# Nineteen small extra loads at the start of a one-core decode kernel that streams a key and value cache

## The chip, the cores and the metric

The kernel runs on one core of a Trainium2 chip. The metric is the time of one execution in microseconds (us), the median of repeated runs. A core has a matrix engine (TensorE, "PE" in the profile), a vector engine (VectorE, "DVE"), a scalar engine (ScalarE, "ACT"), GpSimd ("POOL") and SyncE ("SP"), which here only issues transfers. Sixteen DMA engines move data between the large memory (HBM) and the on-chip buffer (SBUF). An engine issues a transfer with one instruction; the instruction goes on a queue, and the DMA engines work through the queue's pieces ("packets"). In the profile, "SPq" is SyncE's stream of such instructions.

## What is computed

One token goes through two branches, whose results are mixed with a scalar gate. The reference, cut to what matters:

```python
g = sigmoid((x * gate_w).sum(-1))                      # x: 1 x 1 x 448
q = (x @ wq).reshape(16 heads, 256)                    # wq: 448 x 4096
scores = q . k_cache * 256 ** -0.5                     # k_cache: 8 heads x 65536 x 256, bf16
a = (softmax(scores) . v_cache).reshape(4096) @ wo     # two query heads share one key/value head
b = (relu(x @ W_gate) * (x @ W_up)) @ W_down           # 448 -> 1792 -> 448
out = g * a + (1 - g) * b
```

The two caches have 268 MB each. Everything else together is about 12 MB.

## The kernel before

**Tiles.** Each of the 8 key/value heads is cut into 4 tiles of the key cache and 4 of the value cache. A tile is 128 partitions x 32768 bf16 elements, 64 KB in each partition and 8.39 MB in all. There are 64 tiles. Three SBUF buffers, `ring[0]` to `ring[2]`, take the tiles in turn; a tile's load is issued when the buffer's last user is done with it. For a key tile, VectorE transposes blocks in place (line 352, eight pieces), TensorE multiplies with the query (line 364), VectorE takes the maximum (line 501) and ScalarE the exponential (line 503). For a value tile TensorE multiplies with the transposed probabilities (line 395). The last value tile comes in four pieces, and the output weights `wo` are spread over the end (line 579).

**The order of the work.** Each operation is noted with an engine, a due time and its dependencies (`op` and `dma`). At the end each engine's operations are sorted by due time and written out in that order, with waits on counters (semaphores) ahead of an operation that needs another engine's or a transfer's result. So the due time fixes the place in an engine's program, and nothing else. An engine that waits holds up all that comes after it in its own program.

**The start, in SyncE's order.** The order of issue is: `wq` (384 of the 448 rows of the query weights, into `ring[2]`, line 434), the gate and up weights (384 rows each, line 449), `wqh` (the other 64 rows of the query weights, into `ring[1]`, line 435), the first key tile into `ring[0]` (line 495), then the last 64 rows of gate and up as 32 transfers of 4 rows each (`rows64`, line 375), the down weights (`wd`, line 482), and the key tiles 1 and 2. `rows64` waits for `z_f`, a GpSimd memset of the padding (line 243), the first operation in GpSimd's program. `wd` waits for the query product `q` (line 324), because it overwrites the query weights in `ring[2]`. Key tile 1 goes into `ring[1]` and waits for `q` as well, since `wqh` lies there; key tile 2 goes into `ring[2]` and waits for the gated branch (`gu`, `dn`).

**GpSimd at the start.** After `z_f` it makes index and selection tables (lines 260 to 275). The last of them, `selc`, is read by a transpose on TensorE (line 443) right after `q`.

The dictionary `held` lists, for each ring buffer, what must be done before its first tile is loaded.

Of the kernel before, what the change touches and what calls it, by code (L numbers as in the profile page):

```python
# [24 lines left out]
class _Plan:  # L25
# [8 lines left out]
    def op(self, eng, key, fn, deps=()):  # L34
        o = _Op(eng, key, fn, deps)
        self.ops.append(o)
        return o

    def dma(self, eng, key, sem, fn, deps=()):
        if sem not in self.dsem:  # L40
            self.dsem[sem] = self.es.enter_context(self.nc.semaphore("d_" + sem))
        o = _Op(eng, key, fn, deps, dma=sem)
        self.ops.append(o)
        return o
# [46 lines left out]
def bass_gated_mix__gqa_block_cached__glu_gated_reglu__decode_kernel(  # L91
# [38 lines left out]
    with es:  # L130
# [3 lines left out]
        ring = [sb("ring%d" % i, [128, U * DH], BF) for i in range(NRING)]  # L134
# [61 lines left out]
        op, dma = pl.op, pl.dma  # L196
        touch_m = []

        def mop(*a, **k):
            o = op(*a, **k)  # L200
            touch_m.append(o)
            return o
# [18 lines left out]
        t = 3.0  # L221
# [5 lines left out]
        T_END = t + 20.0  # L227


        slot, held, freed = {}, {1: ["q"], 2: ["gu", "dn"]}, {}  # L230
        r = 0
        for kind, i, _ in order:
            if kind in ("k", "v") or (kind, i) in (("wo", 0), ("vp", 0)):
# [145 lines left out]
        l_, qk, smax, aexp, pv, last = {}, {}, {}, {}, {}, {}  # L379
# [52 lines left out]
        for kind, i, t in issue:  # L432
            if kind == "wq":
                l_["wq"] = dma("sp", t, "wq", lambda e: e.dma_start(wq3, A_wq[0:NR3, :].rearrange("(p k) n -> p (k n)", k=R3)))
                l_["wqh"] = dma("sp", t + 0.01, "wqh", lambda e: e.dma_start(
                    wqa, A_wq[NR3:D, :].rearrange("r (c n) -> (r c) n", c=2)))
                tq = tL["wq", 0]
                l_["qm"] = mop("pe", tq, f_q, [l_["wq"], q0])
                l_["q"] = mop("pe", tq + 8, f_q2, [l_["qm"], l_["wqh"]])
# [5 lines left out]
            elif kind == "gu":  # L445
                a1, a2 = [], []
                t = tL["gu", 0]
# [43 lines left out]
            elif kind == "k":  # L491
# [14 lines left out]
                if t_ == NTH - 1:  # L506
# [13 lines left out]
                    for rd in range(2):  # L520
# [18 lines left out]
                        q = op("ac", tt + 1, f_ev, [p, pv.get((h - 1) * NTH - 1)])  # L539
# [103 lines left out]
```

## Time and profile before

| | |
|---|---|
| time, median of 2 runs | 1281.05 us (1280.99 to 1281.1) |
| the profiled execution's own time | 1281.17 us |
| its span, first to last instruction | 1279.9 us |
| read from HBM | 549.03 MB, 429 GB/s over the span |
| PE, DVE, ACT, POOL busy | 33%, 50%, 5%, 1% of the span |

The span is what the profiler saw of the program; 1.27 us of that execution's time lie outside it. The share of a DMA queue is the time that its packets took, as a share of sixteen engines' span. The windows of the profile count a packet in the window in which it starts, so that in a short window the share can be over 1. A transfer's landing is counted from its issue to the last rise of its semaphore.

### The profile page before, as it was taken

To read this page: it belongs to the slowest core of one execution; us is meant where nothing else is said; L and a number is where in the kernel's file an instruction comes from. 1 tells how busy PE (TensorE), PEld (TensorE's weight loads), DVE (VectorE), ACT (ScalarE), POOL (GpSimd) and SP (SyncE) were. 2 spreads that over 40 slices of the span, in tenths; PEclk is the share of its full clock that TensorE was granted. 3 is DMA by queue.
4 is the path that set the end of the run, shared out by engine and by line. 5 is a ranking of instruction groups with operands and counts; after the bars stand their busy time and mean duration, and the time that the engine had idled before them with its cause. 6 is when DMAs were issued, how large, how long until landed. Compare 5 with 4: busy or idle time off the path is not lost.

```text
span 1279.9 us, 10025 instructions
## 1 busy us (share of the span) xinstructions
PE 426.5 (33%) x4634; PEld 159.5 (12%) x4634; DVE 639.1 (50%) x438; ACT 61.5 (5%) x116; POOL 10.5 (1%) x22
## 2 busy tenths in 40 slices
PE   5324323334223431325331343322433314233244
PEld 4201101111001110002110111100111101011021
DVE  2588633565434655345555444555435555336600
ACT  0000000000000000000000000000000000000000
POOL 3000000000000000000000000000000000000000
PEclk8655666656666666666656666656566666666576
DMA  9999999999999999999999999999999999999997
GB/s 410 428 427 447 429 428 433 437 433 429 439 431 431 435 435 426 433 445 427 427 433 440 435 425 431 437 439 427 427 435 441 428 431 435 435 431 437 430 426 334
DMA packets 11936, 549.68 MB, mean 429 GB/s; under 512 B 1395, under 2 KB 1654, under 8 KB 2806
## 3 DMA queue, kind: packets, MB, share of 16 engines
q1 hardware_dynamic: 11890, 549.03, 99.4%
q8 instruction: 36, 0.59, 0.2%
q14 instruction: 6, 0.05, 0.0%
q10 hardware_dynamic: 4, 0.00, 0.0%
HBM read 549.03 MB, written 0.00 MB: 429 GB/s over the span
## 4 chain that ended last, share of the span: by engine, by line
DVE 34%; DMA 31%; another core or an unknown queue 16%; PE 14%; SPq 2%; issue 1%; ACT 1%; POOL 0%; POOLq 0%
DVE ring L352 31%; DMA ring<-in_A_k_cache_dram 27%; PE ST L364 6%; PE O L395 6%; DMA ring<-in_A_wo_dram 3%; DVE P_sb L523 1%; SPq L375 1%; DMA ring<-in_B_W_up_dram 1%; DVE nmb L501 1%; PE PT L528 1%; POOL ring L243 0%; ACT ptp L537 0%; PE M_ps L515 0%; DVE attnT L425 0%
## 5 line engine op out<-in xcount | busy, mean ns | idle before, releaser
L352 DVE STREAM_TRANSPOSE ring<-ring 128x2048 uint32<-128x2048 uint32 x256 | 565.5, 2275 | 408.9 <-DMA ring<-in_A_k_cache_dram 408.9
L364 PE MATMUL ST<-ring,xm 128*16 128x512 bf16 x2048 | 225.5, 614 | 754.0 <-DVE ring L352 754.0
L364 PEld LDWEIGHTS ST<-ring,xm 128*16 128x16 bf16 x2048 | 61.6, 120 | 903.6 <-DVE ring L352 794.6
L395 PE MATMUL O<-ring,ptp 128*4 128x512 bf16 x2048 | 149.2, 455 | 34.6 <-DMA ring<-in_A_v_cache_dram 30.6
L503 ACT ACTIVATE P_sb<-ST,nmb 128x512 bf16<-128x512 f32 x32 | 45.2, 1414 | 1112.0 <-DVE nmb L501 1112.0
L501 DVE TENSOR_REDUCE nmb<-ST 128x1 f32<-128x512 f32 x32 | 22.0, 689 | 109.6 <-PE ST L364 109.6
L395 PEld LDWEIGHTS O<-ring,ptp 128*4 128x4 bf16 x2048 | 54.2, 99 | 129.3 <-issue 60.3
L409 DVE CAST o_sb<-O 128x512 bf16<-128x512 f32 x8 | 5.5, 692 | 78.2 <-PE O L395 78.2
L523 DVE TENSOR_TENSOR P_sb<-P_sb,hs 128x1024 bf16<-128x1024 bf16 x16 | 18.9, 1222 | 8.9 <-ACT hs L517 8.9
L528 PE MATMUL PT<-identb,P_sb 128*128 128x128 bf16 x128 | 16.5, 310 | 15.5 <-DVE P_sb L523 14.7
L528 PEld LDWEIGHTS PT<-identb,P_sb 128*128 128x128 bf16 x128 | 12.3, 140 | 18.3 <-DVE P_sb L523 18.3
L537 ACT COPY ptp<-PT 128x256 bf16<-128x256 bf16 x32 | 10.3, 375 | 23.0 <-PE PT L528 23.0
L317 PE MATMUL M_ps<-ring,P_sb 128*128 128x256 bf16 x48 | 8.3, 357 | 0.7 <-DMA ring<-in_A_wq_dram 0.7
L503 ACT ACTIVATION_READ_ACCUMULATOR P_sb<-ST,nmb 128x1 f32 x32 | 8.5, 267 | 0.0
L467 PE MATMUL M_ps<-xT,ring 48*128 48x1 bf16 x28 | 1.8, 195 | 14.5 <-DMA ring<-in_B_W_up_dram 14.5
L317 PEld LDWEIGHTS M_ps<-ring,P_sb 128*128 128x128 bf16 x48 | 6.0, 127 | 2.8 <-DMA ring<-in_A_wq_dram 0.7
L243 POOL MEMSET ring<- 32x7168 bf16 x1 | 6.1, 6061 | 0.3 <-POOLq L628 0.3
L513 PE MATMUL M_ps<-identf,hs 128*2 128x128 f32 x8 | 2.7, 335 | 10.0 <-DVE hs L511 10.0
L441 DVE STREAM_TRANSPOSE ptp<-P_sb 128x128 uint32<-128x128 uint32 x1 | 0.3, 311 | 11.2 <-ACT P_sb L440 11.2
L459 PE MATMUL M_ps<-xT,ring 128*128 128x1 bf16 x84 | 5.2, 198 | 1.7 <-DVE nselT L444 1.7
L425 DVE TENSOR_SCALAR attnT<-M_ps,hs 64x4 bf16<-64x4 f32 x16 | 3.5, 221 | 3.7 <-PE M_ps L418 3.6
L597 PE MATMUL A_ps<-ring,attnT 128*1 128x224 bf16 x64 | 5.3, 321 | 0.1
(78 smaller groups left out, 82.8 us busy)
## 6 DMA issues: line engine op xcount, KB each, us to landing
ring<-in_A_v_cache_dram SPq DMA_DIRECT2D x1, 4096.0 KB, 27.0
ring<-in_A_wq_dram SPq DMA_DIRECT2D x1, 3072.0 KB, 10.2
ring<-in_A_v_cache_dram SPq DMA_DIRECT2D x1, 2048.0 KB, 31.6
ring<-in_A_v_cache_dram SPq DMA_DIRECT2D x2, 1024.0 KB, 34.6
ring<-in_A_wo_dram SPq DMA_DIRECT2D x4, 448.0 KB, 36.4
ring<-in_B_W_down_dram SPq DMA_DIRECT2D x1, 1568.0 KB, 19.6
ring<-in_B_W_gate_dram SPq DMA_DIRECT2D x1, 1344.0 KB, 13.0
ring<-in_B_W_up_dram SPq DMA_DIRECT2D x1, 1344.0 KB, 15.8
```

Source lines behind the costliest of these rows:

```text
L243: z_f = op("gp", -0.5, lambda e: e.memset(ring[2][0:32, WB - 2 * F:WB + 2 * F], 0.0))
L317: ins = e.matmul(QN_ps, xw3[:, kt, 31 - j:159 - j], wq3[:, kt * NQ + j * 256:kt * NQ + (j + 1) * 256], start=(j == 0 and kt == 0), stop=Fa ...
L352: return lambda e: e.transpose(v, v)
L364: ins = e.matmul(bank[32 * w:32 * w + 16, :], xm[:, x0:x0 + 16], ktv[sl][:, u0:u0 + 16, c, :, r_], start=(b == 0 and c == 0 and r_ == 0), ...
L375: d_ = dma("sp", t + 0.0001 * i, sem, lambda e, i=i, b0=b0, r0=r0: e.dma_start(dsts[i // 8][b0:b0 + 13:4, :], W[r0:r0 + 13:4, :]), deps)
L395: ins = e.matmul(OP[h % 2][32 * g:32 * g + 4, :], ptp[h % 2][:, col:col + 13:4], ring[sl][:, k * 512:(k + 1) * 512], start=(a == 0 and k < ...
L409: e.tensor_copy(dst[:, :, 0:4, :], src)
L501: smax[n] = op("dv", tk + 22, lambda e, n=n, NM=NM, t_=t_: e.tensor_reduce(NM[:, t_:t_ + 1], ST[n % 2][:], AX.X, ALU.max, negate=True), [q ...
L503: aexp[n] = op("ac", tk + 23, lambda e, n=n, t_=t_, NM=NM, RS=RS: e.activation(P_sb[:, t_:2048:4], ST[n % 2][:], ACTF.Exp, bias=NM[:, t_:t ...
L523: rsc = op("dv", tt, lambda e, X=X, pb=pb: e.tensor_tensor(pb, pb, X[:, 12:16].unsqueeze(1).to_broadcast([128, 256, 4]), ALU.mult), [h7, a ...
L528: ins = e.transpose(PT[rd][:, s * 128:(s + 1) * 128], P_sb[:, (rd * 8 + s) * 128:(rd * 8 + s + 1) * 128], identb[:, :])
L537: ins = e.copy(dst, src)
```

## The change

Two groups of loads are added, and nothing reads what they bring.

- `pk`: 15 loads on SyncE's queue. The i-th takes i rows of `wq`, 1024 elements (2 KB) of each, into i partitions of `ring[1]`, beyond the part that `wqh` uses. Their due times lie between 3.0051 and 3.0065; `wq` has 3.0, gate and up have 3.001 and 3.002, `wqh` has 3.01. So in SyncE's program they stand behind the gate and up weights and ahead of `wqh`.
- `pg`: 4 loads on GpSimd's queue, each of 4 rows of `wq` into partitions 64 to 67 of `ring[1]`, with 8, 7, 6 and 5 KB per row. Their due times, -0.9 to -0.87, put them ahead of `z_f` (-0.5), the first operation of GpSimd's program.
- Key tile 1, the first tile in `ring[1]`, additionally waits until both groups have landed.

```diff
-        slot, held, freed = {}, {1: ["q"], 2: ["gu", "dn"]}, {}
+        slot, held, freed = {}, {1: ["q", "pk", "pg"], 2: ["gu", "dn"]}, {}
...
                 l_["wqh"] = dma("sp", t + 0.01, "wqh", lambda e: e.dma_start(
                     wqa, A_wq[NR3:D, :].rearrange("r (c n) -> (r c) n", c=2)))
+                for i in range(1, 16):
+                    l_["pk"] = dma("sp", t + 0.005 + 0.0001 * i, "pk", lambda e, i=i: e.dma_start(
+                        ring[1][0:i, 4096 + i * 1024:4096 + (i + 1) * 1024], A_wq[0:i, 0:1024]))
+                for i in range(4):
+                    l_["pg"] = dma("gp", -0.9 + 0.01 * i, "pg", lambda e, i=i: e.dma_start(
+                        ring[1][64:68, 4096 + i * 4096:8192 + i * 4096 - 512 * i], A_wq[4 * i:4 * i + 4, 0:4096 - 512 * i]))
```

## The prediction

> **What bounds the kernel now.** I read the page's queue part first, then a table of the span by stretches, then SyncE's own waits.
>
> ```profile
> q1 hardware_dynamic: 11890, 549.03, 99.4%
> HBM read 549.03 MB, written 0.00 MB: 429 GB/s over the span
> ```
>
> ```profile
> 2.00:1278.00 1276.00, 426.23 (x4634) 159.50 (x4634) 637.62 (x432) 60.65 (x115) 9.04 (x18) 0.62 1.00 431
> 1270.00:1274.00 4.00, 1.73 (x16) 0.21 (x16) 0.00 (x0) 0.00 (x0) 0.00 (x0) 0.50 0.79 318
> 1274.00:1276.00 2.00, 1.91 (x26) 0.90 (x24) 1.14 (x4) 0.00 (x0) 0.00 (x0) 0.50 0.44 174
> 1276.00:1278.00 2.00, 1.94 (x22) 0.83 (x18) 0.19 (x1) 0.00 (x0) 0.00 (x0) 0.50 0.14 53
> ```
>
> ```profile
> SPq L560 <- PE ST L364: 912.2, 29, 35.0
> ```
>
> SyncE's queue keeps the sixteen DMA engines busy for 99.4% of the span. In the stretches (the last two columns are the DMA share and GB/s) the share is 1.00 from 2 us to 1278 us; the hardware has no idle time to lose except in the last 8 us, where the share falls to 0.79, 0.44 and 0.14: some DMA engines run out of work earlier than others. SyncE itself waits 912.2 us for ring buffers to come free, which looks like the bound and isn't, as the landings show:
>
> ```profile
> ring<-in_A_v_cache_dram SPq DMA_DIRECT2D x31, 36.7
> ```
>
> A tile has 8.39 MB, which takes 8.39 / 0.429 = 19.6 us. A value tile lands 36.7 us after its issue, so it finds some 17 us of other work ahead of it in the queue. While SyncE waits, the DMA engines have work. The time is therefore set by the bytes that the DMA engines must move, plus the start and the end, and the engine with most to do ends last. A delay of an issue costs time only where it is longer than the queue that lies ahead of it.
>
> **The change, part by part.** Nothing is removed. Four things are added or moved.
>
> *1. Work for the DMA engines.* The fifteen `pk` loads have 1 + 2 + ... + 15 = 120 rows of 2048 B, 245,760 B. The four `pg` loads have 4 x (8192 + 7168 + 6144 + 5120) = 106,496 B. Together 0.352 MB, at 429 GB/s 0.82 us if all sixteen engines share it. How unevenly small loads fall is shown by the loads of 4 rows that are there already:
>
> ```profile
> 26.16 17.25 DMA ring<-in_B_W_up_dram
> ```
>
> ```profile
> 6.80 10.04 SPq L375 DMA_DIRECT2D ring<-in_B_W_gate_dram  x16
> 16.88 9.86 SPq L375 DMA_DIRECT2D ring<-in_B_W_up_dram  x16
> 38.79 6.70 DVE L352 STREAM_TRANSPOSE ring<-ring 128x2048 uint32<-128x2048 uint32 x3 [15.10 <-DMA ring<-in_A_k_cache_dram]
> 43.51 1.81 PE L467 MATMUL M_ps<-xT,ring 48*128 48x1 bf16 x28 [14.50 <-DMA ring<-in_B_W_up_dram]
> ```
>
> The first fence is from the chain that ended last, cut to the start; the second is the timeline. The 32 loads of 4 rows are queued behind key tile 0. Vector work on that tile starts at 38.79, so it had landed by then. The small loads have landed at 26.16 + 17.25 = 43.41, 4.62 us later. They hold 32 x 4 x 3584 B = 0.459 MB, which sixteen engines would move in 1.07 us and four engines in 4.28 us. So a load of 4 rows runs on four engines. The rest, 4.62 - 4.28 = 0.34 us over 32 packets on an engine, is 0.011 us of overhead per packet.
>
> If a load of i rows likewise gives one row to each of i engines, always starting from the same one, the first engine gets 15 packets of 2048 B. At 429 / 16 = 26.8 GB/s per engine each takes 0.076 + 0.011 = 0.087 us, in all 1.3 us; the fifteenth engine gets 0.09 us. For `pg` each engine gets at most one 8 KB row if the four loads go to different engines, 0.31 + 0.01 = 0.3 us, and 26,624 B, 1.0 us, if all four go to the same. The existing small loads leave four engines 4.6 us behind, and the falling shares in the last 8 us are what such a lag looks like when it is never made up: with 17 us queued, the other twelve never wait for the slow four, and the end does. If the first engine of `pk` is one of these four, the end moves by **1.3 + 0.3 = 1.6 us**. The ends of this term are 0.8 us (evenly spread) and 1.3 + 1.0 = 2.3 us. I take 1.6, nearest to what the 4-row loads show.
>
> [...] The 4.62 us agree with four engines; which four, no row here shows.
>
> *2. SyncE's issue time.* The nearest rows of issues:
>
> ```profile
> 0.72 0.40 SPq L434 DMA_DIRECT2D ring<-in_A_wq_dram  x1
> 1.63 0.43 SPq L449 DMA_DIRECT2D ring<-in_B_W_up_dram  x1
> 2.11 0.75 SPq L435 DMA_DIRECT2D ring<-in_A_wq_dram  x1
> 2.90 0.44 SPq L495 DMA_DIRECT2D ring<-in_A_k_cache_dram  x1
> 26.79 3.03 SPq L482 DMA_DIRECT2D ring<-in_B_W_down_dram  x1
> 29.86 32.37 SPq L495 DMA_DIRECT2D ring<-in_A_k_cache_dram  x3
> ```
>
> The 32 small issues went from 6.80 to 26.74, 0.62 us each. The 128-partition issues take 0.45 us with the step to the next, `wqh` 0.79. So fifteen `pk` cost between 6.8 and 11.9 us; I take the 4-row rate, 15 x 0.62 = **9.3 us**. `wqh` is then issued at 2.11 + 9.3 = 11.4 (at worst 14.0), key tile 0 at 12.2 (14.8), the small loads from 12.6 (15.2). Is there work in the queue until then?
>
> ```profile
> ring<-in_B_W_up_dram SPq DMA_DIRECT2D x1, 1344.0 KB, 15.8
> ring<-in_A_wq_dram SPq DMA_DIRECT2D x1, 512.0 KB, 16.6
> ```
>
> The up weights land at 1.63 + 15.8 = 17.4 and `wqh` at 2.11 + 16.6 = 18.7. These engines are thus occupied up to about 17 us without either, and key tile 0 is needed some 1.2 us after that. Issues at 11.4 and 12.2 are ahead by 5 us, the worst ones by 3. The query product isn't hurt: its first part runs on TensorE until 19.34, and `wqh` lands at most 1.6 us later than 18.7, with `wd` as its nearest customer more than 10 us away. Cost: nothing, covered by `wq`, gate and up.
>
> The small loads then end at 12.6 + 19.9 = 32.5, `wd` (3.03 us, a long issue that I leave as it is) at 35.6, and key tile 1 is issued at about 35.7 instead of 29.86. Key tile 0 keeps every engine busy until about 38.8 + 0.8, and `wd`'s 1.6 MB for 3.7 us more. Cost: nothing; what is left of the cover is about 4 us on twelve engines, and 4.6 us more on the four that have the small loads.
>
> *3. GpSimd.* No row shows a load issued by GpSimd. The rows around it:
>
> ```profile
> 0.72 6.06 POOL L243 MEMSET ring<- 32x7168 bf16 x1 [0.29 <-POOLq L628]
> 12.16 0.19 POOL L275 TENSOR_SCALAR selc<-selc 128x2 f32<-128x2 f32 x1
> 21.88 0.27 PE L443 MATMUL M_ps<-identf,selc 128*2 128x128 f32 x1 [0.55 <-ACT P_sb L440]
> ```
>
> The memset `z_f` ends at 6.78 now. Behind four issues of X us it ends at 6.78 + 4X. Nearest rows are SyncE's issues: 0.4 to 3.03 us. I take 1 us: `z_f` ends at 10.8, before SyncE gets to the small loads (12.6), so it is hidden behind part 2. At the upper end, X = 3.03, it ends at 18.9 and the small loads end at 38.8. Twelve engines would run dry for about 1 us before `wd`; they are the ones with 4.6 us to spare at the end. So both ends cost nothing. The tables end at 12.35 now and at 16.4 with X = 1; TensorE reads them at 21.88, and at the upper end (24.5) the gate product waits 2.6 us, with its second half waiting for data until 43.51 anyway. Through this I see no cost.
>
> [...]
>
> *4. The added wait.* Key tile 1 waits for `pk` and `pg` too. Behind it on SyncE stand all later tiles. Both groups are issued by 11.4 us and lie ahead of key tile 0 in the queue, so they have landed long before 35.7. Cost: nothing.
>
> **The sum.** 0 + 1.6 + 0 + 0 = +1.6 us on a profiled execution of 1281.17 us (span 1279.9 and 1.27 outside), so 1282.8; the median of the runs shown is 0.12 lower, which gives **1282.6 us**, 0.12% slower. A measurement of this kernel can tell about 2% from no change, so this is no change.
>
> **The rivals.**
>
> *Evenly spread.* If the small loads fall on engines that aren't the last at the end, or rotate, the added bytes alone count: 0.8 us, 1281.9. For it: the order in which engines end isn't in any row. Against it: 4-row loads go to four engines.
>
> *GpSimd is the bound of the start (slower).* Point of decision: the four late engines have work until 43.41 + 1.6 = 45.0. The small loads and then `wd` with its 3.03 us must have been issued by then, which takes 19.9 + 3.03 = 22.9 us, so `z_f` must end by 45.0 - 22.9 = 22, which is X = 3.8 us. From there each us of X costs 4 us: at X = 6 (z_f at 30.8) the loss is 8.8 us, 1291; at X = 10.4 it is 26 us, 1308, over 2%. For it: GpSimd's issue is unseen here and its memset of 32 partitions takes 6.06 us, so GpSimd is slow. Against it: no issue row is above 3.03 us.
>
> *The lag changes the rate (faster).* The `pk` loads set the engines apart in steps of 0.09 us. If engines that read less in step moved more, say 433 instead of 431 GB/s over the whole stream, 549.03 MB would take 1268 instead of 1274 us, and the time would be 1277. The best neighbouring stretches read 433 and 436:
>
> ```profile
> 142.00:182.00 40.00, 11.69 (x128) 3.75 (x128) 18.36 (x9) 1.40 (x2) 0.00 (x0) 0.64 1.00 433
> 182.00:222.00 40.00, 10.88 (x128) 3.47 (x128) 19.03 (x10) 1.42 (x2) 0.00 (x0) 0.63 1.01 436
> 222.00:262.00 40.00, 10.90 (x136) 3.79 (x136) 20.98 (x14) 1.42 (x2) 0.00 (x0) 0.59 0.99 428
> ```
>
> Against it: the 436 is paid back by 428 in the next stretch, with share 1.01 and 0.99, so this is counting at the edges and not a better rate. The engines are also out of step already, by the 4.6 us of the small loads. The same mechanism could cost as much, 1289.
>
> *The loads are dropped or merged*: 1281.05. Each has its own semaphore and key tile 1 waits for it, so I give this next to nothing.
>
> **How the numbers follow.** Forecast (skewed, hidden issues, 1281.8 to 1283.5) 0.55; evenly spread (1281.0 to 1281.8) 0.2; GpSimd as the bound 0.12, of which 0.03 over 2%; changed rate 0.12, split 0.07 faster and 0.05 slower, with 0.01 of each over 2%; dropped 0.01. The range takes in the first two, half of the faster cases and the slower ones up to X = 5.5: 1279.5 to 1289. Faster by over 2%: 0.01; within 2%: 0.95; slower by over 2%: 0.04.
>
> **What would show it.** Right: fifteen new issues on SyncE of about 0.62 us between the up weights and `wqh`, key tile 0 issued near 12 us, key tile 1 near 36 us; the DMA share of the stretches up to 60 us no lower than now; about 0.35 MB more read; the last wait for `wo` some 1.6 us later. Wrong: GpSimd issues over 3.8 us each, with VectorE waiting for key tile 1 much longer than now; a gap in the DMA share near 40 us; or a rate over the whole stream other than 431 GB/s, which no step here would explain.

## The result, and the profile after

The changed kernel took 1289.56 us (1288.52 and 1290.6), the kernel before 1281.05 us (1280.99 and 1281.1). The ratio is 1.0067, with a 95% interval of 1.005 to 1.0083: within the 2% that the prediction took as its bound, but clear of no change. Forecast was +1.6 us, measured +8.5 us, and the upper end of the range, 1289, was passed by half a microsecond. The profiled execution took 1288.52 us with a span of 1287.2 us, 7.35 us more than the one of before.

First the page of the changed kernel.

```profile
q1 hardware_dynamic: 12130, 549.28, 99.4%
q0 software_dynamic: 128, 0.11, 0.0%
HBM read 549.38 MB, written 0.00 MB: 427 GB/s over the span
```

The added 0.35 MB are there (549.38 against 549.03), and the queue's share is the same 99.4%. So the DMA engines aren't idler. Where is the time? The table by stretches tells (columns: from and to, length, busy time and count of PE, PEld, DVE, ACT and POOL, granted clock, DMA share, GB/s). Before:

```profile
2.00:14.00 12.00, 3.91 (x24) 2.85 (x25) 6.52 (x20) 0.99 (x2) 9.04 (x18) 1.00 0.91 385
14.00:28.00 14.00, 11.70 (x122) 9.69 (x121) 1.89 (x10) 0.37 (x1) 0.00 (x0) 0.85 1.11 479
2.00:82.00 80.00, 31.93 (x338) 21.57 (x338) 42.69 (x49) 2.75 (x5) 9.04 (x18) 0.72 1.01 432
82.00:1200.00 1118.00, 356.29 (x3887) 123.75 (x3891) 580.63 (x366) 54.75 (x102) 0.00 (x0) 0.61 1.00 433
```

The same stretches after:

```profile
2.00:14.00 12.00, 0.91 (x9) 0.77 (x9) 9.36 (x20) 1.00 (x2) 11.03 (x17) 1.00 0.91 327
14.00:28.00 14.00, 7.12 (x48) 5.42 (x48) 0.00 (x0) 0.00 (x0) 0.87 (x5) 0.89 1.11 335
2.00:82.00 80.00, 29.91 (x306) 21.07 (x306) 36.59 (x44) 2.77 (x5) 11.90 (x21) 0.69 1.01 395
82.00:1200.00 1118.00, 361.18 (x3915) 124.87 (x3915) 581.81 (x367) 54.62 (x102) 0.00 (x0) 0.62 1.00 433
```

From 82 us to 1200 us both kernels run at 433 GB/s. All of the loss lies before. There the *share* is the same (0.91 and 1.11 in both), and the *rate* is not: 327 instead of 385 GB/s from 2 to 14 us, 335 instead of 479 from 14 to 28 us. The engines are busy with packets that take longer: by the packet records the 256 packets of 10,752 B of the gate and up weights took 404 ns each before and 500 ns on average after, the 128 packets of 4096 B of `wqh` 159 and 377 ns. A busy share can't show this; the column beside it does. Over the first 82 us the shortfall is (432 - 395) GB/s x 80 us = 2.96 MB, at 433 GB/s 6.8 us, and with the 0.8 us for the added bytes it accounts for the 7.35 us. Packets count where they start, so this measure, used for all runs below, is uncertain by about 1 us.

The timeline of the changed kernel shows who was where:

```profile
1.25 2.29 POOL L441 DMA_DIRECT2D ring<-in_A_wq_dram  x4 [0.81 <-POOLq L634]
2.11 5.67 SPq L438 DMA_DIRECT2D ring<-in_A_wq_dram  x15
3.53 6.09 POOL L243 MEMSET ring<- 32x7168 bf16 x1
7.82 0.39 SPq L435 DMA_DIRECT2D ring<-in_A_wq_dram  x1
8.25 0.43 SPq L501 DMA_DIRECT2D ring<-in_A_k_cache_dram  x1
9.64 10.26 SPq L375 DMA_DIRECT2D ring<-in_B_W_gate_dram  x16
19.94 16.62 SPq L375 DMA_DIRECT2D ring<-in_B_W_up_dram  x16
28.05 3.57 PE L324 MATMUL M_ps<-ring,P_sb 128*128 128x256 bf16 x16 [6.45 <-DMA ring<-in_A_wq_dram]
36.61 5.25 SPq L488 DMA_DIRECT2D ring<-in_B_W_down_dram  x1
41.97 30.20 SPq L501 DMA_DIRECT2D ring<-in_A_k_cache_dram  x3
47.34 6.70 DVE L352 STREAM_TRANSPOSE ring<-ring 128x2048 uint32<-128x2048 uint32 x3 [13.35 <-DMA ring<-in_A_k_cache_dram]
```

GpSimd's four issues take 2.29 us in all and SyncE's fifteen 5.67 us, both less than assumed. Key tile 0 is issued at 8.25, far ahead of need. And yet the second part of the query product, which needs `wqh`, starts at 28.05 instead of 19.40, and the work on key tile 0 at 47.34 instead of 38.79. Issuing is early, moving is late. The line before of the second part, to compare:

```profile
19.40 1.92 PE L324 MATMUL M_ps<-ring,P_sb 128*128 128x256 bf16 x16
```

### The profile page after: what moved, and what is told of

It is laid out like the page before. It is cut to its first block, busy times and chain, and to the rows that moved or that the text cites. A ratio compares the mean times of both kernels' runs of the same rounds, so it can differ in the third digit from the quotient of the medians.

```text
span 1287.2 us, 10045 instructions
## 1 busy us (share of the span) xinstructions
PE 428.4 (33%) x4634; PEld 159.8 (12%) x4634; DVE 641.9 (50%) x438; ACT 61.4 (5%) x116; POOL 12.8 (1%) x26
## 3 DMA queue, kind: packets, MB, share of 16 engines
q1 hardware_dynamic: 12130, 549.28, 99.4%
HBM read 549.38 MB, written 0.00 MB: 427 GB/s over the span
## 4 chain that ended last, share of the span: by engine, by line
DVE 34%; DMA 31%; another core or an unknown queue 16%; PE 14%; SPq 3%; issue 1%; ACT 1%; POOL 1%; POOLq 0%
DVE ring L352 31%; DMA ring<-in_A_k_cache_dram 27%; PE ST L364 6%; PE O L395 6%; DMA ring<-in_A_wo_dram 2%; DMA ring<-in_B_W_up_dram 2%; DVE P_sb L529 1%; SPq L375 1%; SPq L585 1%; DVE nmb L507 1%; PE PT L534 1%; POOL ring L243 0%; ACT ptp L543 0%; PE M_ps L521 0%
## 6 DMA issues: line engine op xcount, KB each, us to landing
ring<-in_A_wq_dram SPq DMA_DIRECT2D x1, 3072.0 KB, 13.7
ring<-in_B_W_down_dram SPq DMA_DIRECT2D x1, 1568.0 KB, 19.5
```

## The experiments

The median of the kernel before was 1281.13 to 1281.22 us in the four groups of runs; each cost is counted from the median of its own group. "Packet records" are the trace's list of DMA packets, with start, duration and size of each. Theories: **P**, placing: rows sent to neighbouring partitions get in each other's way and slow all sixteen engines. (The expectations speak of a write path that such rows share. That is the theory's supposition; the runs show times and rates, not a path.) **S**, source: the loads read the same few rows of `wq` again and again. **I**, issue: the added issues cost. **W**: a load issued by GpSimd costs by itself. **Q**, added later: the fifteen loads cost more when the engines get to them out of step.

### Which group, and is it the place?

The changed kernel, unaltered:

> The changed kernel once more, unaltered, for its spread. All theories: 1288 to 1291 us, near 327 GB/s in the stretch from 2 to 14 us and near 335 GB/s from 14 to 28 us (before: 385 and 479).

It took 1289.83 us (1289.56 to 1290.75), ratio 1.0068 (1.0053 to 1.0083).

The fifteen SyncE loads alone: the four `pg` loads are deleted.

```diff
-        slot, held, freed = {}, {1: ["q", "pk", "pg"], 2: ["gu", "dn"]}, {}
+        slot, held, freed = {}, {1: ["q", "pk"], 2: ["gu", "dn"]}, {}
-                    l_["pg"] = dma("gp", ...
```

> Only the fifteen loads on SyncE. Theory P (placing: rows sent to neighbouring partitions share a write path of the on-chip buffer, which backs up and slows all sixteen DMA engines): the stretch from 2 to 14 us recovers to near 385 GB/s, the one from 14 to 28 us stays near 340; 1281.05 + 1.3 for the bytes on the first engine + 4.2 + 0.5 = about 1287 us. Theory S (source: the loads read the same few rows of wq again and again, and HBM is slow on them) and theory I (issue: the fifteen issues and the late key tile are what costs) expect the same here. The theory of the prediction, bytes alone: 1282.4 us.

1284.33 us, ratio 1.0025 (1.0016 to 1.0035): +3.2 us, less than P's 1287 and more than the 1282.4 of bytes alone.

The four GpSimd loads alone: the `pk` loads are deleted.

```diff
-        slot, held, freed = {}, {1: ["q", "pk", "pg"], 2: ["gu", "dn"]}, {}
+        slot, held, freed = {}, {1: ["q", "pg"], 2: ["gu", "dn"]}, {}
-                    l_["pk"] = dma("sp", ...
```

> Only the four loads on GpSimd. Theory P: four rows go to four neighbouring partitions, so the stretch from 2 to 14 us stays near 327 GB/s and the one from 14 to 28 us recovers to near 470; 1281.05 + 0.3 + 1.6 = about 1283 us. Theory S expects the same. Theory I, by which SyncE's issues cost: 1281.3 us. Bytes alone: 1281.3 us.

1284.02 us, ratio 1.0021 (1.0011 to 1.0031): +2.9 us, somewhat more than P's 1283. No issue is added on SyncE here, so theory I fails for this group.

Both groups, each row to every fourth partition instead of the next one:

```diff
-                        ring[1][0:i, 4096 + i * 1024: ...
+                        ring[1][0:4 * i - 3:4, 4096 + i * 1024: ...
-                        ring[1][64:68, 4096 + i * 4096: ...
+                        ring[1][64:77:4, 4096 + i * 4096: ...
```

> Both groups with the same number of loads, rows, bytes, sources and queues, but their rows go to every fourth partition (0, 4, 8, ... and 64, 68, 72, 76) instead of to neighbours. Theory P: both stretches recover, to at least 375 GB/s from 2 to 14 us and 450 from 14 to 28 us, and the time is that of the bytes, 1282 to 1283.5 us. Theories S and I: unchanged, 1288 to 1291 us and 327 and 335 GB/s.

1285.01 us, ratio 1.003 (1.0018 to 1.0042). The same loads, rows, bytes, sources and queues cost 3.9 instead of 8.7 us: more than half of the loss was the place in the buffer. It isn't P's 1282 to 1283.5 either. The stretches, first of the fifteen alone, then of the four alone, then of both spread:

```profile
2.00:14.00 12.00, 4.05 (x24) 2.96 (x25) 6.53 (x20) 1.00 (x2) 9.04 (x18) 1.00 0.89 380
14.00:28.00 14.00, 8.08 (x52) 5.58 (x49) 1.53 (x9) 0.37 (x1) 0.00 (x0) 0.77 1.10 394
2.00:82.00 80.00, 32.98 (x338) 21.91 (x338) 39.40 (x47) 2.77 (x5) 9.04 (x18) 0.66 1.00 415
```

```profile
2.00:14.00 12.00, 0.90 (x9) 0.76 (x9) 9.38 (x20) 1.00 (x2) 11.03 (x18) 1.00 0.94 305
14.00:28.00 14.00, 10.10 (x78) 7.81 (x79) 1.89 (x10) 0.37 (x1) 0.91 (x5) 1.00 1.09 463
2.00:82.00 80.00, 31.27 (x338) 21.23 (x338) 42.11 (x47) 2.77 (x5) 11.93 (x22) 0.71 1.01 418
```

```profile
2.00:14.00 12.00, 1.37 (x12) 1.13 (x13) 9.37 (x20) 0.99 (x2) 11.03 (x17) 1.00 0.89 343
14.00:28.00 14.00, 10.26 (x76) 7.71 (x75) 1.89 (x10) 0.37 (x1) 0.91 (x5) 1.00 1.11 445
2.00:82.00 80.00, 30.76 (x330) 21.34 (x334) 41.44 (x47) 2.76 (x5) 11.93 (x21) 0.71 1.00 418
```

Each group slows its own stretch: GpSimd's loads the first, SyncE's the second. Two things stay open: alone they cost 3.2 + 2.9 = 6.1 us, together 8.7; and the spread version still has a shortfall, of 445 against 479 GB/s in the second stretch.

### Place against source, with equal loads

The loads of 1 to 15 rows are uneven, so fifteen loads of 8 rows take their place (again 120 rows of 2 KB, no GpSimd loads).

```diff
-                        ring[1][0:i, 4096 + i * 1024:4096 + (i + 1) * 1024], A_wq[0:i, 0:1024]))
+                        ring[1][0:8, 4096 + i * 1024:4096 + (i + 1) * 1024], A_wq[0:8, 0:1024]))
```

> No GpSimd loads; the fifteen SyncE loads all have 8 rows of 2 KB (the same 120 rows and 245,760 B), sent to partitions 0 to 7. Theory P (placing): partitions 0 to 3 share one write path and 4 to 7 the next, so eight engines crowd on two paths; about as slow as the fifteen loads alone, 1283.5 to 1286 us, and the stretch from 2 to 82 us near 415 GB/s (before: 432). Theory S (source rows read again and again): the same. Bytes alone: 1281.7 to 1282.4.

1286.16 us, ratio 1.004 (1.0026 to 1.0055), just above P's 1286.

```diff
-                        ring[1][0:8, ...
+                        ring[1][0:29:4, ...
```

> As the kernel with eight neighbouring rows, but the rows go to partitions 0, 4, 8, ... 28; loads, bytes, source and issue order are the same. Theory P: each engine has a write path of its own, the slow stretch is gone: 1281.7 to 1282.4 us, and 428 GB/s or more from 2 to 82 us. Theories S and I (issue): no change against the neighbouring rows, 1283.5 to 1286 us.

1283.65 us, ratio 1.002 (1.0011 to 1.0029), 2.5 us faster by nothing but the place. But not the 1282.4 at most that P gave.

```diff
-                        ring[1][0:8, ...], A_wq[0:8, 0:1024]))
+                        ring[1][0:8, ...], A_wq.rearrange("r (c n) -> (r c) n", c=4)[8 * i:8 * i + 8, :]))
```

> As the kernel with eight neighbouring rows, destination included, but each load reads 16 KB of its own, in one piece, from wq, instead of 2 KB out of each of the same eight rows. Theory P: no change against it, 1283.5 to 1286 us. Theory S: recovers, 1281.7 to 1282.4 us.

1286.07 us, ratio 1.0038 (1.0024 to 1.0052): with neighbouring partitions the source makes no difference in the time. Later both edits were made together:

> Fifteen loads of 8 rows to partitions 0, 4, ... 28, as in the run with spread rows, and with the source of the other run, 16 KB in one piece for each load. If reading the same eight rows again and again is what is left of the slow stretch: 424 GB/s or more from 2 to 82 us and 1282.2 to 1283.0 us. If it is something else: 419 to 422 GB/s and 1283.4 us or more.

1282.98 us, ratio 1.0015 (1.0006 to 1.0025), within what was expected if the source is the rest. The first 82 us of the four, in the order of this section:

```profile
2.00:82.00 80.00, 30.91 (x322) 21.32 (x326) 37.43 (x46) 2.75 (x5) 9.04 (x18) 0.66 1.01 407
```

```profile
2.00:82.00 80.00, 32.78 (x338) 21.89 (x338) 39.65 (x47) 2.77 (x5) 9.03 (x18) 0.69 0.99 420
```

```profile
2.00:82.00 80.00, 31.41 (x326) 21.66 (x330) 37.94 (x46) 2.77 (x5) 9.04 (x18) 0.67 1.01 410
```

```profile
2.00:82.00 80.00, 31.89 (x338) 21.43 (x338) 40.72 (x48) 2.76 (x5) 9.04 (x18) 0.67 1.01 429
```

By the time, the destination is the larger part (2.5 of the 3.2 us that both edits save), and the source a smaller one that shows only once the destination is out of the way. In the packet records both hold the packets up: the 120 packets of 2 KB take 250 ns each on average with neighbouring partitions and the same rows, 200 ns with the destination spread alone, 218 ns with the source changed alone, and 84 ns with both; 84 ns is what the fastest packets take in all four. The fifteen issues are the same in all four, so theory I is left with no more than the 1.8 us of the last. The edit of the source changed two things, repeated reading and the step between rows (2 KB instead of 8 KB); which of them matters wasn't tried. Nor does the same source always cost as much: in the run with both groups spread, the fifteen's packets read the same rows with the same step and took 102 ns on average.

### How much four partitions take

Thirty loads of 4 rows, all into partitions 0 to 3, again 245,760 B:

```diff
-                for i in range(1, 16):
+                for i in range(30):
-                        ring[1][0:i, 4096 + i * 1024:4096 + (i + 1) * 1024], A_wq[0:i, 0:1024]))
+                        ring[1][0:4, 2048 + i * 1024:2048 + (i + 1) * 1024], A_wq[0:4, 0:1024]))
```

> No GpSimd loads; thirty SyncE loads of 4 rows of 2 KB, all into partitions 0 to 3, the same 245,760 B. Theory P: one write path has to take all of it, at an engine's 27 GB/s 9 us, against 4.5 us on each of two paths with eight rows, so the slow stretch is longer: slower than the eight neighbouring rows' 1286.2, 1287 to 1290 us. If it were the number of engines that crowd which counts: four engines instead of eight do less harm, 1283 to 1285.5 us.

1290.38 us, ratio 1.0072 (1.0056 to 1.0088), a little above P's range.

```profile
14.00:28.00 14.00, 3.94 (x35) 3.25 (x33) 0.00 (x0) 0.00 (x0) 0.00 (x0) 0.75 1.06 255
2.00:82.00 80.00, 29.43 (x306) 20.94 (x306) 33.40 (x44) 2.76 (x5) 9.06 (x18) 0.68 1.00 393
```

Fewer rows come at a time, 4 in a load instead of 8, and it is the slowest of all: here the cost goes with the bytes that one group of four partitions must take. The fullest group takes 245,760 B here, 122,880 B with the eight neighbouring rows and 110,592 B (54 rows) with the fifteen alone; from the first to the last 2 KB packet 9.3, 5.1 and 3.9 us pass, and the cost is 9.2, 5.0 and 3.2 us. For the thirty loads that is 245,760 B / 9.27 us = 26.5 GB/s, about one sixteenth of the whole; for the eight neighbouring rows, in two such groups, 245,760 B / 5.1 us = 48 GB/s. From 21 to 25 us the packet records give a flat 139 GB/s for all sixteen engines together, though a load of 4 rows keeps only four of them busy: in the kernel before, never more than four of the 128 packets of 3584 B of the existing 4-row loads are at work at once.

By what way four partitions hold up all sixteen engines, no run shows; shown are the 26.5 GB/s that they took and the 139 GB/s of all engines meanwhile.

### GpSimd's queue, or its destination?

The four loads alone, rows to sixteen different groups of four partitions:

```diff
-                        ring[1][64:68, 4096 + i * 4096: ...
+                        ring[1][(0, 16, 64, 80)[i]:(0, 16, 64, 80)[i] + 13:4, 4096 + i * 4096: ...
```

> Only the four loads on GpSimd, with the same rows and bytes, but their rows go to partitions 0, 4, 8, 12 (first load), 16 to 28, 64 to 76 and 80 to 92, sixteen different groups of four partitions. Theory P, if the four loads take four different sets of four engines: 1281.3 to 1281.7 us and 428 GB/s or more from 2 to 82 us. Theory W (a load issued by GpSimd slows the engines by itself, wherever it goes): 1282.4 us or more and 424 GB/s or less. Neighbouring partitions gave 1284.0 us and 418 GB/s.

1282.61 us, ratio 1.0012 (1.0002 to 1.0021), and 423 GB/s over the first 82 us: half of the 2.9 us is gone, against P's nearly all and W's none.

```profile
2.00:82.00 80.00, 31.68 (x338) 21.20 (x338) 43.60 (x48) 2.77 (x5) 11.88 (x21) 0.68 1.00 423
```

The neighbouring partitions again, but issued by SyncE:

```diff
-                    l_["pg"] = dma("gp", -0.9 + 0.01 * i, "pg", ...
+                    l_["pg"] = dma("sp", t + 0.005 + 0.0001 * i, "pg", ...
```

> The four loads of the GpSimd group alone, same rows and neighbouring partitions, issued by SyncE behind the up weights. Theory P: the place and not the queue is what costs, so 1282.5 to 1284.5 us (by GpSimd: 1284.0). Theory W (GpSimd's issuing is what costs): 1281.3 to 1281.8 us.

1285.34 us, ratio 1.0032 (1.002 to 1.0044), even slower than by GpSimd, and above P's range.

```profile
2.00:82.00 80.00, 32.53 (x326) 22.07 (x330) 38.10 (x46) 2.76 (x5) 9.06 (x18) 0.70 1.00 410
```

So the cost doesn't need GpSimd's queue. That the place makes it is shown by a run further below, in which seven loads of 4 rows (8 KB each), issued by SyncE to partitions 32, 36, 40 and 44, leave the rate at 431 GB/s; the four here bring it to 410. What the other 1.5 us of the matched loads are isn't settled: 0.25 us are bytes.

### Why the two together cost more than their sum

The fifteen unaltered, GpSimd's four to sixteen groups of partitions:

```diff
-                        ring[1][64:68, 4096 + i * 4096: ...
+                        ring[1][32 + 16 * i:45 + 16 * i:4, 4096 + i * 4096: ...
```

> The changed kernel with its fifteen SyncE loads unaltered and GpSimd's four loads sent to sixteen different groups of four partitions (32 to 44, 48 to 60, 64 to 76, 80 to 92 in steps of four). The two groups alone cost 3.2 and 2.9 us, together 8.7, so 2.6 are unexplained. Theory Q (GpSimd's loads into one group of partitions put the sixteen engines out of step, and the SyncE loads then crowd for longer): most of the 2.6 go; the two alone cost 3.2 + 1.5 = 4.7, so 1285.8 us, 1285 to 1287. If merely having both queues at work makes the excess: 1287.5 us or more.

1288.22 us, ratio 1.0053 (1.0035 to 1.0071). The excess over the sum, 7.0 - 3.2 - 1.5 = 2.3 us, stayed. Theory Q in this form was wrong: it isn't the crowding of GpSimd's loads. The rival that was named, that both queues at work are enough, fits this run. To see whether being out of step is enough, without GpSimd, seven loads of 4 x 8 KB were put ahead of the fifteen, on four partitions in steps of four. At the rates worked out in the prediction (26.8 GB/s for one engine, 0.011 us more per packet) 7 x 8192 B keep each of four engines busy some 2.2 us longer, an estimate.

```diff
+                for i in range(7):
+                    l_["ps"] = dma("sp", t + 0.004 + 0.0001 * i, "ps", lambda e, i=i: e.dma_start(
+                        ring[1][32:45:4, 2048 + i * 4096:6144 + i * 4096], A_wq[4 * i:4 * i + 4, 0:4096]))
                 for i in range(1, 16):
```

> No GpSimd loads. [...] Theory Q: being out of step is enough; the stretch from 2 to 82 us falls well below the 415 GB/s of the fifteen alone, to 405 or less. If the order in which engines arrive doesn't matter: 413 to 417 GB/s, and 1284.3 plus 0.5 to 2.2 us for the added bytes = 1284.8 to 1286.5 us.

1288.91 us, ratio 1.006 (1.0044 to 1.0076). And these seven alone:

> Only the seven loads of 4 rows that were put ahead of the fifteen in the run with engines out of step (partitions 32, 36, 40, 44). If they are nearly free: 428 GB/s or more from 2 to 82 us, and 0.5 to 2.2 us for the bytes, 1281.7 to 1283.4 us; the out-of-step excess is then real. If they cost by themselves what the out-of-step run was slower by: 417 GB/s or less, and 1284.5 us or more.

1283.09 us, ratio 1.0015 (1.0006 to 1.0025). The first 82 us, of the run out of step and of the seven alone:

```profile
2.00:82.00 80.00, 29.42 (x306) 20.79 (x306) 34.29 (x45) 2.75 (x5) 9.06 (x18) 0.67 1.00 399
```

```profile
2.00:82.00 80.00, 33.07 (x338) 21.74 (x338) 40.45 (x48) 2.75 (x5) 9.04 (x18) 0.66 1.01 431
```

The seven take nothing from the rate (431 against 432); their 1.9 us are near the 2.2 us estimated for their bytes on four engines. The fifteen alone have 415 GB/s. Together 399: a shortfall of 6.1 us where the parts have 3.1 + 0.2. So loads that take nothing from the rate by themselves make the fifteen take twice as much, and GpSimd's queue isn't needed for it. In the packet records the fifteen loads' packets start within 16.1 to 19.7 us when alone, within 16.1 to 24.7 us behind the seven, and within 17.4 to 24.9 us in the changed kernel.

That the four late engines are the reason is not shown by these two runs. The seven's own 57,344 B in each of four partitions are an estimated 2.2 us at the measured 26.5 GB/s; whether those are part of the 5 us by which the fifteen's packets take longer (up to 24.7 instead of 19.7 us), no run shows. In the changed kernel the loads ahead were done in time: GpSimd's last packet ended at 13.7 us, and the first of the fifteen's started at 17.4. There something that the earlier loads leave behind makes the excess; the order in which the engines arrive is the author's guess, and only argued.

Last, both groups with GpSimd's after the others:

```diff
-                    l_["pg"] = dma("gp", -0.9 + 0.01 * i, "pg", lambda e, i=i: e.dma_start(
+                    l_["pg"] = dma("gp", 3.02 + 0.01 * i, "pg", lambda e, i=i: e.dma_start(
...
-                        ... A_wq[4 * i:4 * i + 4, 0:4096 - 512 * i]))
+                        ... A_wq[4 * i:4 * i + 4, 0:4096 - 512 * i]), [l_["wqh"]])
```

> Both groups, all places and sizes unaltered, but GpSimd issues its four loads only when wqh has landed, so that they come behind the fifteen and the engines are in step when they get to these. Theory Q: no excess, 3.2 + 2.9 = 6.1, so 1287.3 us (1286.5 to 1287.8), and from 14 to 28 us more than the changed kernel's 324 to 335 GB/s. If the two groups make an excess in any order: 1289 us or more.

1287.0 us, ratio 1.0046 (1.0029 to 1.0063). The number is near Q's 1287.3, but the profile doesn't let it count as that. The stretch of the fifteen is nearly as with these alone (382 against 394 GB/s, the changed kernel 335), and their packets start within 16.1 to 19.5 us, as alone. So the excess on the fifteen needs loads ahead of them; that agrees with Q, and speaks against both queues being enough in any order. But the rest of the time has another source, which the stretches and SyncE's waits show:

```profile
14.00:28.00 14.00, 8.18 (x52) 5.68 (x50) 1.24 (x7) 0.37 (x1) 2.29 (x4) 0.77 1.08 382
42.00:54.00 12.00, 3.49 (x56) 3.43 (x56) 7.05 (x6) 0.00 (x0) 0.00 (x0) 0.50 0.88 352
```

```profile
SPq L83 <- DMA ring<-in_A_wq_dram: 8.3, 1, 8.3
```

GpSimd's loads now land so late that key tile 1 waits 8.3 us for them, and the DMA engines run dry: a share of 0.88 from 42 to 54 us. It is the one run in which the added wait costs, and the price is mostly a lower share, not a lower rate at full share.

## Why the prediction was wrong

- **What bounds the kernel: right.** The time follows the bytes. What is lost in the first 82 us is never made up; the 433 GB/s from 82 to 1200 us are the same in all runs.
- **Part 1, work for the DMA engines: the step that failed.** It priced a small load at an engine's own rate, 0.087 us per 2 KB, and let it delay only the engine that carries it, between 0.8 and 2.3 us in all. The runs showed instead that small loads delay all sixteen engines when their rows go to neighbouring partitions: 8.7 us for both groups, 3.9 with the rows spread. The fifteen alone cost 3.2 us; the four alone 2.9 us, of which the place accounts for half; both together 2.6 us more than that, because the fifteen's slow stretch lasts longer behind other loads. Why it does is open. How the rows of the added loads fall on the engines, on which the 1.3 and the 0.3 us of the sum rest, no run shows; these 3.2 and 2.9 us stand in their place. The existing 4-row loads, which gave the price, write every fourth partition (`b0:b0 + 13:4` in the code); the added ones write neighbours. The prediction took no account of that difference. Where the rows were placed and sourced well, the loads cost 1.8 us for the fifteen, near the 1.3 us of the working.
- **Part 2, SyncE's issues: wrong in size, right in effect at first.** 0.38 us each instead of 0.62, so `wqh` went out at 7.82 instead of 11.4. Later the issues took longer, while the queue was late: the sixteen `up` loads took 16.62 us instead of 9.86, `wd` 5.25 instead of 3.03, and key tile 1 went out at 41.97 instead of the 35.7 of the prediction. The cover held nearly (a share of 0.99 from 42 to 54 us), because key tile 0 was late too. That `wqh` lands at most 1.6 us later was wrong, as its customer on TensorE started 8.65 us later; `wd`, issued at 36.61, had no need of it earlier.
- **Part 3, GpSimd: right that the issuing costs nothing.** It was 2.29 / 4 = 0.57 us per issue, inside the bounds and below the 1 us taken. `z_f` wasn't hidden behind part 2: SyncE was ready for the small loads at 8.68 and began them at 9.64, when `z_f` had ended at 9.62. That 1 us was covered by the queue.
- **Part 4, the added wait: right** for the change (the group that follows `wqh` in one of the runs shows what it costs when it isn't covered).
- **The rivals.** *GpSimd as the bound*, *evenly spread* and *dropped* (0.35 MB more were read) fell. *The lag changes the rate* named a changed rate, but over the whole stream and as likely up as down; its 1289 for the slow side is near the measured time by chance, since the rate from 82 to 1200 us didn't change. The case that came true, a slower rate for a few microseconds at the place of the loads, wasn't among them.

## What to carry to other kernels

In a kernel that keeps its DMA engines busy all the time, price a transfer by where its rows land as well as by its bytes: rows in four neighbouring partitions went at 26.5 GB/s in all, and everything else slowed down meanwhile. Here small loads of a few rows were cheapest on every fourth partition with a source read once, in one piece (84 ns per 2 KB packet against 250, and 1.8 us for fifteen loads against 5.0). And read the rate beside the busy share: here a share that stayed (1.11 from 14 to 28 us) with a falling rate (479 to 335 GB/s) meant packets that took longer, and a falling share (0.88 from 42 to 54 us, GpSimd's loads after the others) meant a late issue.

## What the runs showed of the hardware that was not expected

- One group of four partitions that takes 26.5 GB/s held the sixteen engines together at 139 GB/s, instead of some 430.
- Loads that cost no rate (431 against 432 GB/s) doubled what others behind them took from it (399 against 415 for these alone). Whether late engines or something else does this is open; a full explanation would also have to cover that placing GpSimd's loads well left 2.3 us of the excess, and that issuing them after the fifteen took it from the fifteen's stretch.
- Reading the same rows again and again with a step of 8 KB costs too (200 against 84 ns per 2 KB packet, 0.7 us of time), but with neighbouring partitions it made no difference in the time (250 against 218 ns).
- In the changed kernel one SyncE issue of 4 rows, the last before `wd`, took far longer than the 0.58 us of its neighbours; the view of that line gives 6709 ns as the longest, against 577 before. That it waited for a queue that was behind is likely, and not shown:

```profile
L375 SPq DMA_DIRECT2D ring<-in_B_W_up_dram x16: 576/577/6709, 19.9 to 29.9; - x16
```
